# Shifting the tiles between two MLP matrices inside their buffers, and streaming half of them backward into TensorE

## The chip, the cores and the metric

The kernel runs on one core of one Trainium2 chip. The metric is the device time of one execution in microseconds; the kernel before takes 642.31 us (median of 3 runs, 641.87 to 642.67). TensorE (PE) multiplies, VectorE (DVE) and ScalarE (ACT) do elementwise work, GpSimd (POOL) helps, SyncE (SP) issues the DMAs. SBUF is the on-chip memory that all engines read, PSUM the one that TensorE writes.

## The reference, cut to what matters

Three stages run one after the other on a batch of 2 with 448 positions and 768 channels: capped softmax attention (12 heads of 64), then a Fourier mixing with a residual, a layer norm and an MLP, then a gated MLP over positions. The change lies in the MLP of the second stage alone:

```
X = np.fft.fft(np.fft.fft(x, axis=1), axis=2)
u = x + np.real(X)
un = (u - mean(u)) / sqrt(var(u) + 1e-6)
ch = np.maximum(un @ w_ch1, 0.0) @ w_ch2      # 768 -> 3072 -> 768
x = u + ch
```

## The kernel before

All activations are kept transposed: channels on the 128 partitions, the 448 positions of one batch as columns. A channel vector of 768 is six such tiles. Products are made to float32 accuracy out of a pair of tiles in the type fp32r, a high part and a low part: `product` (L134) issues three matmuls for each chunk of the contraction, high by high, high by low and low by high. In each of them the weights are the stationary operand (128 by 128) and the activations the moving one, which is streamed column by column: 448 columns. Every matmul has its own weight load (LDWEIGHTS).

The MLP has 3072 hidden channels, 24 chunks of 128. They are done in six groups `g` of four chunks (`GF = 4`). For one group, `hidden(b, g, ...)` (L719) makes the four hidden chunks of batch `b`: 18 matmuls each into PSUM (`h<-un,w` in the trace). From PSUM, ACT writes the high part with the ReLU (L727), and DVE the low part (L728), into a tile `h` of 2 by 512 columns of which the first 448 are used. Then `mixed(b, g, ...)` (L731) multiplies: for each of the six output chunks `c`, 12 matmuls with `h` as the moving operand and a block of the second matrix as weights (`c<-h,w`), into one PSUM tile of 512 columns, and DVE adds the 448 used columns to the residual (L736). `b` is 0 or 1, so a group has 144 matmuls `h<-un,w` and 144 matmuls `c<-h,w`. `hidden` and `mixed` serve the groups 1 to 5. Group 0 goes through `hidden_parts` and `mixed_parts` (L741 to L778), which are written out by hand between the Fourier stage and the layer norm of batch 1, and which have their own tiles `h`.

The order in each group is: `hidden` of batch 0, `hidden` of batch 1, `mixed` of batch 0, `mixed` of batch 1 (L1131 to L1162). Outside the written-out parts a scheduler places the instructions. The tiles `h` have four buffers for each batch, that is one group's worth. Weights come by DMA as raw 64-bit words (L670) and are converted on ACT and DVE (L685 to L693) and split into high and low parts (L131, L132) while TensorE works on the group before.

Other streams that the prediction reads: the f32 (not fp32r) products of attention, `o<-e,v` (L556) and `den<-e,ones` (L567); the f32 products of the Fourier stage, `st<-t,fold` (L221), whose moving operand is a table of three rows of 194 columns, so that its streams begin at columns 0, 194 and 388; the gate's `v<-wv,x` with 256 moving columns (L140); DVE's reversed copy `back<-pq` (L232), which reads 768 columns with step -1; and the four additions of the Fourier stage (L249 to L252), of which L250 and L252 walk through `xT` with step -1 and begin at column 1 of the PSUM tile, while L249 and L251 go forward.

Of the kernel before, what the change touches and what calls it, by code (L numbers as in the profile page):

```python
# [13 lines left out]
F32R = mybir.dt.float32r  # L14
# [7 lines left out]
P = 128  # L22
B, H, S, D = 2, 12, 448, 64
# [7 lines left out]
GF = NF // NG  # L31
# [25 lines left out]
W_BUFS = {"wa": 4, "wb": 4, "wc": 2}  # L57


FILL = {"const": 160, "wb": 96, "normed0": 224, "hidden0": 96, "wc": 96}  # L60
EDGE, GATE_ROW, TABLE_ROW = 160, 192, 3776

# [23 lines left out]
def f32(ap):  # L86
    return ap.bitcast(F32)
# [3 lines left out]
def attention_mixers_kernel(ctx, tc, bounded, q, k, v, cap, w_ch1, w_ch2, w_in, g_ln, w_sg, b_sg, w_out,  # L91
# [10 lines left out]
    def fill(pool, name):  # L102
        t = pool.tile([P, FILL[name] // 4], F32, tag="fill", bufs=1, name=f"fill_{name}")
        nc.gpsimd.memset(t[:, 0:1], 0.0)
# [4 lines left out]
    def big_ps(name):  # L109
        pool, n = banks[-1]  # L110
        return pool.tile([P, 2, 512], F32, tag="big", bufs=n, name=name)
# [3 lines left out]
    def one_ps(name):  # L115
        if not ring:
            return banks[-1][0].tile([P, 512], F32, tag="one", bufs=4, name=name)
        ring.append(ring.pop(0))
        pool, tag, n = ring[-1]
        return pool.tile([P, 512], F32, tag=tag, bufs=n, name=name)  # L120
# [8 lines left out]
    def split(hi, lo, src, lo_engine=None, hi_copy=None):  # L129

        (hi_copy or act.copy)(hi, src)  # L131
        (lo_engine or vec).tensor_tensor(lo, src, f32(hi), op=ALU.subtract)  # L132

    def product(ps, lhs, rhs, n, start=True, stop=True):  # L134

        last = 3 * n - 1
        m = 0
        for i in range(n):
            for a, b in ((0, 0), (0, 1), (1, 0)):
                pe.matmul(ps, lhs(i, a), rhs(i, b), start=start and m == 0, stop=stop and m == last)  # L140
                m += 1
# [572 lines left out]
    def rows(src, f0, name, tag="wb", **how):  # L714

        return weight(f"{name}{f0}", row_block(src, f0), 1, C, tag, **how)


    def hidden(b, g, un, w1, hs, chunks=range(GF)):  # L719
        for f0 in chunks[::2]:  # L720
            ps = big_ps(f"h{b}_{g}_{f0}")
            for i in range(2):
                product(ps[:, i, :S], lambda n, a: w1[f0 + i][:, a, n, :], lambda n, a: un[b][:, a, n, :], NP)
                yield
            for i in range(2):
                h = hpool[b].tile([P, 2, 512], F32R, tag="h", bufs=4, name=f"h{b}_{g}_{f0 + i}")[:, :, :S]
                act.activation(h[:, 0], ps[:, i, :S], AF.Relu)  # L727
                vec.scalar_tensor_tensor(h[:, 1], ps[:, i, :S], 0.0, f32(h[:, 0]), op0=ALU.max, op1=ALU.subtract)  # L728
                hs.append(h)

    def mixed(b, g, hs, w2, x2):  # L731
        u = xT[b]
        for c in range(NP):
            ps = one_ps(f"c{b}_{g}_{c}")
            product(ps[:, :S], lambda n, a: w2[n][:, a, c * P:(c + 1) * P], lambda n, a: hs[n][:, a, :], GF)
            vec.tensor_tensor(u[:, c, :], u[:, c, :], ps[:, :S], op=ALU.add)  # L736
            if x2 is not None:
                split(x2[:, 0, c, :], x2[:, 1, c, :], u[:, c, :])
            yield

    def hidden_parts(b, g, un, w1, hs):  # L741

        ps = {}

        def prod(f, rows=range(NP), idles=0):

            if f not in ps:
                t = big_ps(f"h{b}_{g}_{f}")
                stream(t[:, 0], idles)
                for i in range(2):  # L750
                    ps[f + i] = t[:, i, :S]
            for n in rows:
                product(ps[f], lambda _, a: w1[f][:, a, n, :], lambda _, a: un[b][:, a, n, :], 1,
                        start=n == 0, stop=n == NP - 1)

        def relu(f):
            h = hpool[b].tile([P, 2, 512], F32R, tag="h", bufs=4, name=f"h{b}_{g}_{f}")[:, :, :S]
            act.activation(h[:, 0], ps[f], AF.Relu)
            vec.scalar_tensor_tensor(h[:, 1], ps[f], 0.0, f32(h[:, 0]), op0=ALU.max, op1=ALU.subtract)
            hs.append(h)  # L760

        return SimpleNamespace(prod=prod, relu=relu)
# [103 lines left out]
    def opened(*names):  # L866
        pools = [ctx.enter_context(tc.tile_pool(name=name, bufs=1)) for name in names]
        for pool, name in zip(pools, names):
            if name in FILL:
                fill(pool, name)  # L870
# [15 lines left out]
    with ExitStack() as fctx:  # L886
# [8 lines left out]
        with ExitStack() as actx:  # L895
# [6 lines left out]
            w1, w2, w1_next = [], [], []  # L902
            side = iter(())
            if bounded:
                f, n0 = fourier(0, fp, t2sb, POOL_FOLDS[0]), layer_norm(0, fp)
# [83 lines left out]
        hpool = [None, None]  # L989
# [13 lines left out]
        if bounded:  # L1003
            normed[0] = opened("normed0")
            with tc.manual_schedule():
# [5 lines left out]
                hs = []  # L1011
# [69 lines left out]
                h = hidden_parts(1, 0, un, w1, hs1)  # L1081
# [19 lines left out]
        else:  # L1101
# [3 lines left out]
            def main_steps():  # L1105
                hs = []
                yield from hidden(0, 0, un, w1, hs)
                yield from mixed(0, 0, hs, w2, None)
                yield from hidden(0, 1, un, w1_next, hs_next[0], range(2))
# [11 lines left out]
    if not bounded:  # L1121
        hpool[1] = ctx.enter_context(tc.tile_pool(name="hidden1", bufs=1, side="right"))
        run(hidden(1, 0, un, w1, hs1))
    if not bounded:
        run(mixed(1, 0, hs1, w2, None))
# [5 lines left out]
    for g in range(1, NG):  # L1131
        if g == 1:
# [3 lines left out]
            hs = hs_next  # L1136
# [3 lines left out]
        else:  # L1140
            w1 = [columns(w_ch1, g * GF + f, "w1_") for f in range(GF)]
            hs = [[], []]
            for b in range(B):
                run(hidden(b, g, un, w1, hs[b]))
        if g == 3:
            for c in range(NT):
                sg_raw = sp_pool.tile([P, S], F32, tag="sgraw", bufs=1, name=f"sg_raw{c}")[:CP]
                sp.dma_start(sg_raw, w_sg[c * CP:(c + 1) * CP, :])
                ps = one_ps(f"sgT{c}")
# [8 lines left out]
        w2 = [rows(w_ch2, g * GF + f, "w2_") for f in range(GF)]  # L1158
        for b in range(B):
            if g == NG - 1:  # L1160
                x2[b] = normed[b].tile([P, 2, NP, S], F32R, tag="normed", name=f"x2_{b}")
            run(mixed(b, g, hs[b], w2, x2[b]))  # L1162
# [54 lines left out]
```

## Time and profile before

| | |
|---|---|
| median of 3 runs (lowest, highest) | 642.31 us (641.87, 642.67) |
| span of the profiled execution, first to last instruction | 641.1 us |
| PE busy | 621.4 us, 97% |
| weight loads (PEld) busy | 536.5 us, 84% |
| DVE busy | 502.7 us, 78% |
| ACT busy | 273.5 us, 43% |
| POOL busy | 82.9 us, 13% |
| `h<-un,w`, 864 matmuls | 175.3 us of PE |
| `c<-h,w`, 864 matmuls | 175.4 us of PE |

The profiled execution is known by its span alone; the three timed runs are others. Their median lies 1.2 us over the span, which is taken for what lies around the first and the last instruction. Weight loads overlap matmuls, so PE and PEld don't add up. The trace gives a matmul's start as measured, and its end as modelled: a duration of 363 ns is longer than the distance to the next start. The rate of a stream is therefore read from the chain of waits, where a stretch of so many matmuls in a row has one length.

### The profile page before, as it was taken

Reading aid. Unit: us, or ns where it says so; the run is one execution under the profiler, and the core shown is the slowest. Engines: PE = TensorE matmul, PEld = TensorE weight load, DVE = VectorE, ACT = ScalarE, POOL = GpSimd, SP = SyncE. Lnnn points to the kernel's source line nnn. Section 1 sums busy time; section 2 is a strip of 40 time slices with the busy share of each in tenths; the row PEclk is TensorE's granted clock in tenths of the full one; section 3 lists DMA queues with packets and bytes.
Section 4 is the critical chain, followed back from the end, with each engine's and each line's share of the span. In section 5 each row is a group of like instructions: output and inputs, shape, how many; then the busy total and the mean of one; then the engine's idle time right before and its main releaser. Section 6 shows DMA issues by size and latency. Waiting matters only on the chain.

```text
span 641.1 us, 8759 instructions
## 1 busy us (share of the span) xinstructions
PE 621.4 (97%) x3414; PEld 536.5 (84%) x3414; DVE 502.7 (78%) x733; ACT 273.5 (43%) x374; POOL 82.9 (13%) x82
## 2 busy tenths in 40 slices
PE   7899999999999999999999999999999999999995
PEld 5444576559988999999999989999999999999995
DVE  1899999989985789998957882698589789997451
ACT  3998875671312244333403530352245244533121
POOL 1555564353000000000000000000000000101000
PEclk9999999999999999999999999999999999999998
DMA  6754820400401144544522360145054214000123
GB/s 164 185 135 102 244 61 15 139 0 2 147 2 28 50 147 154 174 157 138 167 99 70 128 204 32 48 151 173 23 153 143 99 50 149 1 1 1 44 58 78
DMA packets 69618, 62.74 MB, mean 98 GB/s; under 512 B 35840, under 2 KB 63296, under 8 KB 69568
## 3 DMA queue, kind: packets, MB, share of 16 engines
q1 hardware_dynamic: 68640, 61.86, 31.9%
q8 instruction: 29, 0.48, 0.3%
q10 hardware_dynamic: 928, 0.23, 0.2%
q14 instruction: 21, 0.17, 0.1%
HBM read 59.32 MB, written 2.75 MB: 97 GB/s over the span
## 4 chain that ended last, share of the span: by engine, by line
PE 83%; DVE 10%; DMA 2%; ACT 2%; issue 1%; POOLq 0%; POOL 0%; DVEq 0%; ACTq 0%; SPq 0%
PE c L140 26%; PE h L140 24%; PE v L140 5%; PE out L140 5%; PE u L140 4%; PE s L532 4%; PE o L556 4%; PE sg L140 3%; DVE r L576 2%; PE st L242 1%; DMA sg_raw<-in_moe_w_sg 1%; PE st L221 1%; PE tr L501 1%; ACT e L537 1%; PE idle L152 1%
## 5 line engine op out<-in xcount | busy, mean ns | idle before, releaser
L140 PE MATMUL h<-un,w 128*128 128x448 f32 x864 | 175.3, 363 | 0.5 <-DVE un L325 0.5
L140 PE MATMUL c<-h,w 128*128 128x448 f32 x864 | 175.4, 363 | 0.0
L140 PEld LDWEIGHTS h<-un,w 128*128 128x128 f32 x864 | 161.7, 188 | 12.4 <-DVE un L325 0.8
L140 PEld LDWEIGHTS c<-h,w 128*128 128x128 f32 x864 | 161.9, 188 | 11.1 <-issue 0.4
L736 DVE TENSOR_TENSOR xT<-xT,c 128x448 f32<-128x448 f32 x60 | 36.9, 617 | 37.2 <-PE c L140 37.2
L820 POOL TENSOR_TENSOR bag<-bag,neg_half 112x1 f32<-112x1 f32 x8 | 6.0, 745 | 396.5 <-DVE bag L819 396.5
L537 ACT ACTIVATE e<-s,tanh_scale 128x896 f32<-128x896 f32 (+1 forms) x48 | 41.1, 921 | 19.6 <-PE s L532 19.2
L556 PE MATMUL o<-e,v 128*64 128x448 f32 x192 | 41.1, 551 | 0.0
L541 ACT ACTIVATE e<-e,cap_pos 128x1792 f32<-128x1792 f32 (+1 forms) x24 | 37.7, 1620 | 0.0
L140 PE MATMUL v<-wv,x 128*112 128x256 f32 x288 | 34.2, 280 | 0.0
L140 PEld LDWEIGHTS v<-wv,x 128*112 128x112 f32 x288 | 34.1, 175 | 0.1
L727 ACT ACTIVATE h<-h 128x448 fp32r<-128x448 f32 x40 | 21.7, 542 | 28.7 <-DVE h L728 19.8
L532 PE MATMUL s<-qT,kT 64*128 64x448 f32 x216 | 27.5, 383 | 6.3 <-DVE qT L510 5.2
L576 DVE RECIPROCAL r<-den 128x448 f32<-128x448 f32 x11 | 32.4, 2948 | 0.8 <-PE den L569 0.7
L532 PEld LDWEIGHTS s<-qT,kT 64*128 64x128 f32 x216 | 19.3, 185 | 16.1 <-DVE qT L510 6.9
L140 PE MATMUL out<-gated,wo 128*128 128x448 f32 x144 | 30.8, 367 | 0.0
L140 PE MATMUL u<-x,wu 128*128 128x448 f32 x144 | 29.1, 362 | 0.0
L548 POOL TENSOR_TENSOR t<-t,e 128x896 f32<-128x896 f32 x12 | 28.6, 2381 | 0.8
L140 PEld LDWEIGHTS u<-x,wu 128*128 128x128 f32 x144 | 27.0, 188 | 1.8
L545 POOL TENSOR_TENSOR t<-e 128x896 f32<-128x896 f32 x12 | 27.8, 2320 | 2.7 <-POOL mix L521 1.7
L140 PEld LDWEIGHTS out<-gated,wo 128*128 128x128 f32 x144 | 26.4, 188 | 1.8 <-ACT res L861 0.2
L556 PEld LDWEIGHTS o<-e,v 128*64 128x64 f32 x192 | 11.8, 136 | 17.6 <-issue 15.2
(380 smaller groups left out, 900.7 us busy)
## 6 DMA issues: line engine op xcount, KB each, us to landing
k<-in_k SPq DMA_DIRECT2D x24, 112.0 KB, 2.8
out<-res SPq DMA_DIRECT2D x12, 224.0 KB, 2.5
q<-in_q SPq DMA_DIRECT2D x22, 112.0 KB, 2.8
t<-dft_channels SPq DMA_DIRECT2D x8, 291.0 KB, 5.1
v<-in_v SPq DMA_DIRECT2D x24, 96.0 KB, 2.3
w_0raw<-in_moe_w_ch SPq DMA_DIRECT2D x2, 768.0 KB, 5.0
w_1raw<-in_moe_w_ch SPq DMA_DIRECT2D x2, 768.0 KB, 6.0
w_2raw<-in_moe_w_ch SPq DMA_DIRECT2D x2, 768.0 KB, 4.7
```

The source lines that it names most:

```text
L140: pe.matmul(ps, lhs(i, a), rhs(i, b), start=start and m == 0, stop=stop and m == last)
L152: pe.matmul(ps[:, 0:2 * P], idle[:, 0:P], idle, start=True, stop=True)
L221: pe.matmul(ps[:HS, m * 256:m * 256 + NE], fold[:, i, m * HS:(m + 1) * HS], tab[:, i, :], start=i == 0, stop=i == 2)
L532: pe.matmul(ps[:, i, :S], t[lo:hi, x, at:at + P], qT[lo:hi, y, :], start=m == 0, stop=m == 2)
L537: act.activation(es[n][:, 2 * step:2 * step + nr], sums.pop((n, step))[:, :nr, :S], AF.Tanh, scale=tanh_scale)
L541: act.activation(part, part, AF.Exp, scale=cap_pos)
L545: pool.tensor_tensor(t, es[n][:, 0:2], es[n][:, 2:4], op=ALU.add)
L548: pool.tensor_tensor(ts[n], ts[n], es[n][:, 4:6], op=ALU.add)
L556: pe.matmul(os[n][halfs[j], :S], vts[n % 3][:, j, i], es[n][:, 2 * i + j if i < 3 else 6], start=i == 0, stop=i == 3)
L576: vec.reciprocal(r, den[:, :S])
L727: act.activation(h[:, 0], ps[:, i, :S], AF.Relu)
L736: vec.tensor_tensor(u[:, c, :], u[:, c, :], ps[:, :S], op=ALU.add)
```

## The change

Two edits, in `hidden` and in `mixed`, thus in the groups 1 to 5.

First, a tile `h` of group 1 or later no longer starts at column 0 of its 512. A table of twenty numbers gives the starting column by group and chunk: 0, 4, 8 and so on to 60 in steps of four for the first sixteen, then 2, 6, 1 and 18 for the four chunks of group 5. Both batches use the same numbers. ACT and DVE write the tile there and TensorE reads it there. A column has 4 bytes.

Second, for batch 1 of the groups 1 to 5 both the moving operand and the PSUM output of the matmuls `c<-h,w` are addressed from the last column to the first, with step -1. Each result lands where it did before.

```
+H_AT = (0, 4, 8, 12, 16, 20, 24, 28, 32, 36, 40, 44, 48, 52, 56, 60, 2, 6, 1, 18)
...
             for i in range(2):
-                h = hpool[b].tile([P, 2, 512], F32R, tag="h", bufs=4, name=f"h{b}_{g}_{f0 + i}")[:, :, :S]
+                at = H_AT[GF * (g - 1) + f0 + i] if g else 0
+                h = hpool[b].tile([P, 2, 512], F32R, tag="h", bufs=4, name=f"h{b}_{g}_{f0 + i}")[:, :, at:at + S]
                 act.activation(h[:, 0], ps[:, i, :S], AF.Relu)
                 vec.scalar_tensor_tensor(h[:, 1], ps[:, i, :S], 0.0, f32(h[:, 0]), op0=ALU.max, op1=ALU.subtract)
...
             ps = one_ps(f"c{b}_{g}_{c}")
-            product(ps[:, :S], lambda n, a: w2[n][:, a, c * P:(c + 1) * P], lambda n, a: hs[n][:, a, :], GF)
+            back = -1 if b and g else 1
+            product(ps[:, :S][:, ::back], lambda n, a: w2[n][:, a, c * P:(c + 1) * P],
+                    lambda n, a: hs[n][:, a, ::back], GF)
             vec.tensor_tensor(u[:, c, :], u[:, c, :], ps[:, :S], op=ALU.add)
```

No instruction moves on any engine: DVE, ACT, POOL and SP have the same instructions in the same order with the same waits. On TensorE the matmuls stand in the same order too, and 11 places get a wait on TensorE's own semaphore (`PE_49`). Nine are the first matmuls of output chunks 1, 2 and 3 of batch 0 in the groups 2, 4 and 5; two are transposes of the gate's matrix in group 3. Here is TensorE in the program before, where `mixed` of batch 0 in group 2 begins its second output chunk (`c0_2_1` is batch 0, group 2, chunk 1; the names end in a running number):

```order
L140 MATMUL c0_2_0_2690<-h0_2_3_2557,w2_11_2682 128x448 x2
L140 MATMUL c0_2_1_2704<-h0_2_0_2511,w2_8_2649 128x448 x3
L140 MATMUL c0_2_1_2704<-h0_2_1_2514,w2_9_2660 128x448 x3
L140 MATMUL c0_2_1_2704<-h0_2_2_2554,w2_10_2671 128x448 x3
L140 MATMUL c0_2_1_2704<-h0_2_3_2557,w2_11_2682 128x448 x3
L140 MATMUL c0_2_2_2718<-h0_2_0_2511,w2_8_2649 128x448 x3
```

The same place now (the line is L141, since the table added one):

```order
L141 MATMUL c0_2_0_2690<-h0_2_3_2557,w2_11_2682 128x448 x2
L141 MATMUL c0_2_1_2704<-h0_2_0_2511,w2_8_2649 128x448 [waits PE_49]
L141 MATMUL c0_2_1_2704<-h0_2_0_2511,w2_8_2649 128x448 x2
L141 MATMUL c0_2_1_2704<-h0_2_1_2514,w2_9_2660 128x448 x3
L141 MATMUL c0_2_1_2704<-h0_2_2_2554,w2_10_2671 128x448 x3
L141 MATMUL c0_2_1_2704<-h0_2_3_2557,w2_11_2682 128x448 x3
L141 MATMUL c0_2_2_2718<-h0_2_0_2511,w2_8_2649 128x448 [waits PE_49]
```

Nothing moved; the first matmul of a chunk has a wait. It waits for the last user of the same PSUM tile on TensorE, a chunk of `mixed` of batch 1 in the group before, which stands more than 140 matmuls earlier.

## Rows read from the trace of the kernel before

**Rows 1.** Head of the page: busy time of each engine, TensorE's slices and clock

```profile
PE 621.4 (97%) x3414; PEld 536.5 (84%) x3414; DVE 502.7 (78%) x733; ACT 273.5 (43%) x374; POOL 82.9 (13%) x82
...
PE   7899999999999999999999999999999999999995
...
PEclk9999999999999999999999999999999999999998
```

**Rows 2.** Chain of waits in order of time: start, length (us), what, how many

```profile
255.37 28.80 PE c L140 x144
284.17 28.91 PE h L140 x144
313.08 28.80 PE c L140 x144
341.88 28.81 PE h L140 x144
371.11 2.89 DMA sg_raw<-in_moe_w_sg
...
431.53 28.80 PE c L140 x144
460.33 28.81 PE h L140 x144
489.14 28.80 PE c L140 x144
...
532.36 16.92 PE v L140 x144
```

**Rows 3.** Stretches of the groups 2 to 5: length, busy (count) by engine, clock, DMA

```profile
284.00:342.00 58.00, 58.00 (x291) 54.20 (x290) 44.46 (x65) 18.08 (x26) 0.00 (x0) 1.00 0.38 125
460.00:518.00 58.00, 58.00 (x292) 54.38 (x291) 47.33 (x72) 23.68 (x36) 0.00 (x0) 1.00 0.35 109
```

**Rows 4.** Costliest groups on TensorE: count, busy us, mean ns, idle before

```profile
L140 PE MATMUL c<-h,w 128*128 128x448 f32 x864 | 175.4, 363 | 0.0
L140 PE MATMUL h<-un,w 128*128 128x448 f32 x864 | 175.3, 363 | 0.5 <-DVE un L325 0.5
```

**Rows 5.** TensorE's Fourier products, three starting columns: ns min/median/max, first and last start

```profile
L221 PE MATMUL st<-t,fold x96: 325/327/420, 81.8 to 165.6; 128*113 128x194 f32 x96
```

**Rows 6.** The slower streams of 448 columns on TensorE, columns as in rows 4

```profile
L567 PE MATMUL den<-e,ones 128*64 128x448 f32 x48 | 11.2, 544 | 0.4 <-DVE r L576 0.4
```

**Rows 7.** DVE forward and with step -1, columns as in rows 5

```profile
L131 DVE CAST w<-w_1cvt x1: 552/552/552, 42.4 to 42.4; 128x768 fp32r<-128x768 f32 x1
...
L232 DVE COPY back<-pq x4: 550/553/2440, 99.8 to 168.1; 113x768 f32<-113x768 f32 x4
...
L249 DVE TENSOR_TENSOR xT<-xT,st x12: 376/380/393, 102.2 to 177.2; 128x225 f32<-128x225 f32 x12
...
L250 DVE TENSOR_TENSOR xT<-xT,st x12: 373/378/381, 102.5 to 177.5; 128x223 f32<-128x223 f32 x12
```

**Rows 8.** What ACT and DVE do to the tiles `h`, columns as in rows 5

```profile
L727 ACT ACTIVATE h<-h x40: 517/545/557, 235.6 to 490.7; 128x448 fp32r<-128x448 f32 x40
L728 DVE SCALAR_TENSOR_TENSOR h<-h,h x40: 615/617/625, 237.0 to 491.7; 128x448 fp32r<-128x448 f32 x40
```

**Rows 9.** A semaphore instruction of TensorE's queue, columns as in rows 5

```profile
L221 PEldq EVENT_SEMAPHORE  x8: 51/51/2537, 80.9 to 161.5; - x8
```

## Prediction

> **What bounds the kernel now.** Read the head of the page first: TensorE is busy for 621.4 of 641.1 us, its slices are full from the second on, and the granted clock is full in all of them but the last [rows 1]. Then read the chain of waits in order of time. In the MLP it holds nothing but TensorE: 144 matmuls of `h<-un,w`, 144 of `c<-h,w`, and so on, 28.8 us each, broken only by three short waits for a DMA in group 3 [rows 2]. [...] So in groups 1 to 5 the time is the number of matmuls by the distance from one start to the next, and anything that ACT or DVE do has spare time. The distance is 28.80 us / 144 = 200.0 ns for `c<-h,w` and 28.81 / 144 = 200.1 ns for `h<-un,w` [rows 2]. Over the whole kernel the two kinds are alike too: 175.4 and 175.3 us for 864 each [rows 4].
>
> **The change part by part.** It removes and moves nothing. What it alters is how an operand is addressed. I take five parts.
>
> *Streams that start elsewhere.* In five groups there are 5 x 144 = 720 matmuls `c<-h,w`. One start of twenty is still column 0, so 684 read from a shifted column, with the same 448 columns and the same weights. No row has an fp32r stream with such a start. The nearest is `st<-t,fold`: a table of three rows of 194 columns, so a third of its 96 streams each starts at column 0, 194 and 388; 194 is even but no multiple of four. Their durations are 325 at the least, 327 in the median [rows 5], and a stalled start would show here, because the 420 does. Half of all lie within 2 ns of the least although two thirds start off column 0. I take 0. For the bounds I use two fp32r rows: 256 columns take 16.92 us / 144 = 117.5 ns, 448 take 200.0 [rows 2], so a column costs 82.5 / 192 = 0.430 ns, and 117.5 - 256 x 0.430 = 7.4 ns are left per matmul beside the columns. At best a better start takes all of that away: 684 x 7.4 ns = -5.1 us. At worst it is paid a second time: +5.1 us.
>
> *The one tile at column 1.* Of the starts 2, 6, 1 and 18 only the 1 is odd: 3 matmuls by 6 chunks by 2 batches = 36. If columns went to TensorE in aligned pairs, these would fall apart. The slowest 448-column stream in the trace has a mean of 544 ns against 363 [rows 4, 6], so +181 ns; at worst 36 x 181 ns = +6.5 us, at best 0 (already in the -5.1). I take 0: DVE's additions that begin at column 1 of PSUM take 378 ns for 223 columns, those from column 0 take 380 for 225 [rows 7]. It is another engine, so the upper end stays in mind.
>
> *Streams that run backward.* Batch 1 has 5 x 72 = 360 of them, 360 x 200.0 ns = 72.0 us of the chain. Moving operand and output both have step -1. No row shows TensorE with a negative step, so this is the unknown that matters. Below: 0, since the columns are the same number and the stretch is already 448 columns at 0.430 ns plus 7.4. Above: the slow stream's +181 ns on each, 360 x 181 ns = +65.2 us. The nearest rows with a negative step are DVE's. Its reversed copy of 768 columns takes 553 ns in the median and 550 at the least, the forward one of as many 552 [rows 7]. 552 / 768 = 0.72 ns per column, well under the 617 / 448 = 1.38 of a DVE pass that reads PSUM [rows 8], so this is a fast path, and step -1 doesn't lose it. The additions with step -1 through `xT` tie with the forward ones as well [rows 7]. I take 0.
>
> [...]
>
> *Writes of the tiles.* 40 times ACT writes a shifted tile and 40 times DVE does, 545 and 617 ns [rows 8]. An odd start may cost something there. What covers it: the last tile of batch 0 is written while batch 1's 72 matmuls `h<-un,w` run, that of batch 1 while batch 0's 72 `c<-h,w` run, 72 x 0.2 = 14.4 us each, and a PSUM tile of two chunks is wanted back only after the other one's 36 matmuls, 7.2 us. Doubled to 1.1 and 1.2 us they would still be hidden. Cost 0; without the cover, 40 x 0.55 us would show at most for each doubling, 22 us on ACT.
>
> *Waits on TensorE's own semaphore.* 11 waits, each for a matmul more than 140 places back, thus 140 x 0.2 = 28 us old. Behind a waiting matmul all of TensorE stands, and behind it DVE's addition; but the value is long there. An instruction of TensorE's queue for a wait takes 51 ns when it need not wait [rows 9]. Two of the places, the transposes, wait for a DMA anyway [rows 2]. At most 11 x 51 ns = 0.6 us, at least 0; since the queue runs ahead of the matmuls, I take 0.1.
>
> **Sum.** 0 + 0 + 0 + 0 + 0.1 us on the profiled span: 641.1 + 0.1 = 641.2. The median of the runs shown is 642.31, 1.2 us over that span, so 642.4.
>
> **Rivals.**
>
> *Rival 1, slower by much: backward streams run at half rate.* Place: the 72.0 us of batch 1's `c<-h,w`. Mechanism: TensorE takes or writes two neighbouring columns at once and does so only upward, so that each column becomes an access of its own. Price up to 360 x 181 ns = 65.2 us: 642.3 + 65.2 = 707.5. It decides from 1.28 us / 360 = 3.6 ns per backward matmul. [...] Against it: DVE's fast copy, which keeps its rate backward [rows 7].
>
> *Rival 2, slower by a little: a start or a turn has a fixed price.* Every shifted stream pays up to another 7.4 ns: 642.4 + 5.1 = 647.5, with the middle at 645. A backward stream that only begins late belongs here too: 15 ns on 360 are 5.4 us, the same size. It decides from 1.28 / 684 = 1.9 ns per shifted matmul. For it: no fp32r row has a start like these, and the odd one may cost 6.5 us alone. Against it: the even 325 to 327 ns of `st<-t,fold` [rows 5].
>
> *Rival 3, faster: the present starts are the bad ones.* Tiles and weights at like places could get in each other's way, and twenty different starts would break that up. All of the 7.4 ns gone on 684 matmuls is 5.1 us: 642.3 - 5.1 = 637.2. For it: 7.4 ns that no column explains. Against it: `un` and `h` are different tiles in different pools with the same 200.0 and 200.1 ns [rows 2], so where a tile lies has not mattered so far.
>
> **How the numbers follow.** No change 0.63, rival 1 0.12, rival 2 0.15, rival 3 0.10. A difference under 0.2% (1.28 us) can't be told from none here. So faster 0.10, same 0.63, slower 0.12 + 0.15 = 0.27. The likeliest case's own range is 641.0 to 643.6. The range given is 639.5 to 647.7: it holds no change, rival 2 to its end and half of rival 3, together about 0.83, and leaves out rival 1, whose price lies far off.
>
> **What would show it.** Right: in the chain of waits the stretches of 144 `c<-h,w` in groups 1 to 5 stay at 28.8 us, TensorE stays at 58.00 of 58.00 with clock 1.00, and no new wait of TensorE for itself is listed. Rival 1: such a stretch grows to some 40 us, and its second half, batch 1, has starts near 380 ns apart while the first half keeps 200. Rival 2: both halves grow by a few ns each, or only the 36 matmuls of the odd tile in group 5 do. Rival 3: both halves fall towards 193 ns. The writes at L727 and L728 should keep 545 and 617 ns. I am wrong if TensorE's distances in batch 1's half differ from 200 ns by 4 or more, or if TensorE waits where it did not.

## The result, and the profile after

The changed kernel takes 645.73 us (median of 3 runs, 645.70 to 646.15) against 642.31 us before: 1.0057 of the time, 95% interval 1.0037 to 1.0076, thus 3.4 us slower. The profiled execution has a span of 643.5 us.

The costliest groups on TensorE, columns as in rows 4:

```profile
L141 PE MATMUL c<-h,w 128*128 128x448 f32 x864 | 178.8, 367 | 0.0
L141 PE MATMUL h<-un,w 128*128 128x448 f32 x864 | 175.2, 362 | 1.5 <-DVE d L322 1.0
```

They answer to [rows 4]: `h<-un,w` keeps its 175 us, `c<-h,w` has 3.4 us more, with no idle time before it. The chain of waits shows where; start, length in us, what, how many:

```profile
227.43 28.81 PE h L141 x144
256.24 29.35 PE c L141 x144
285.59 28.81 PE h L141 x144
314.40 29.55 PE c L141 x144
343.94 28.81 PE h L141 x144
...
383.18 26.00 PE c L141 x127
...
433.60 29.45 PE c L141 x144
463.05 28.80 PE h L141 x144
491.85 29.69 PE c L141 x144
521.54 14.40 PE u L141 x72
```

Three more lines of the chain before, for comparison here and below (batch 1 of group 0, the 127 of group 3, the first `u`):

```profile
212.15 14.40 PE c L140 x72
...
381.69 25.43 PE c L140 x127
...
517.95 14.41 PE u L140 x72
```

Beside [rows 2], every stretch of 144 `c<-h,w` has grown: by 0.55, 0.75, 0.65 and 0.89 us in groups 1, 2, 4 and 5; the 127 of group 3 took 25.43 us before, +0.57. That makes 3.41 us, as much as the medians differ (3.42). The two profiled spans differ by 2.4 us only: the changed one reaches group 1's `c<-h,w` 0.9 us later, spends 0.6 us less on the waits between the two stretches of group 3, and ends 1.2 us sooner after its last ACT instruction. These three lie outside the stretches of `c<-h,w`, and no run ties them to the change. `h<-un,w` stays at 28.8. In a stretch the first 72 matmuls are batch 0 (forward), the last 72 batch 1 (backward). Worked out from the start of each matmul (in group 3 without the places where a wait cuts in), the mean distances are 201.7, 204.8, 203.3, 203.8 and 205.1 ns in batch 0 of groups 1 to 5, and 206.0, 205.6, 205.5, 205.3 and 207.2 ns in batch 1, against 200.0 in all ten before. Summed over 72 matmuls each: 1.3 us from batch 0, 2.1 us from batch 1. Both parts of the change cost, and both by a few ns per matmul.

Two stretches that answer to [rows 3], groups 2 and 5, then the writes of the tiles [rows 8]:

```profile
285.60:343.60 58.00, 58.00 (x288) 53.74 (x288) 42.37 (x62) 17.92 (x25) 0.00 (x0) 1.00 0.36 123
463.50:521.50 58.00, 58.00 (x287) 53.79 (x286) 46.58 (x71) 23.18 (x35) 0.00 (x0) 1.00 0.32 109
```

```profile
L729 ACT ACTIVATE h<-h x40: 521/546/556, 236.2 to 493.4; 128x448 fp32r<-128x448 f32 x40
```

```profile
L730 DVE SCALAR_TENSOR_TENSOR h<-h,h x40: 615/618/625, 237.6 to 494.4; 128x448 fp32r<-128x448 f32 x40
```

TensorE waits for nobody and its clock is full, but in 58 us it starts 3 and 5 matmuls fewer than before. ACT and DVE write the shifted tiles as fast as ever.

### The profile page after: what moved, and what is told of

The parts are those of the page before. It is cut to its first block, busy times and chain, and to the rows that moved or that the text cites. A ratio compares the mean times of both kernels' runs of the same rounds, so it can differ in the third digit from the quotient of the medians.

```text
span 643.5 us, 8761 instructions
## 1 busy us (share of the span) xinstructions
PE 624.5 (97%) x3414; PEld 536.4 (83%) x3414; DVE 504.0 (78%) x733; ACT 274.1 (43%) x374; POOL 82.5 (13%) x82
## 4 chain that ended last, share of the span: by engine, by line
PE 84%; DVE 10%; ACT 2%; DMA 1%; issue 1%; POOLq 0%; POOL 0%; DVEq 0%; ACTq 0%; SPq 0%
PE c L141 26%; PE h L141 24%; PE v L141 5%; PE out L141 5%; PE u L141 4%; PE s L533 4%; PE o L557 4%; PE sg L141 3%; DVE r L577 2%; PE st L243 1%; PE st L222 1%; PE tr L502 1%; DVE xT L578 1%; ACT e L538 1%; PE xt L863 1%
## 5 line engine op out<-in xcount | busy, mean ns | idle before, releaser
L141 PE MATMUL c<-h,w 128*128 128x448 f32 x864 | 178.8, 367 | 0.0
L141 PE MATMUL h<-un,w 128*128 128x448 f32 x864 | 175.2, 362 | 1.5 <-DVE d L322 1.0
L141 PEld LDWEIGHTS c<-h,w 128*128 128x128 f32 x864 | 162.3, 188 | 14.1 <-issue 0.4
L141 PEld LDWEIGHTS h<-un,w 128*128 128x128 f32 x864 | 161.7, 187 | 13.4 <-DVE d L322 1.8
L729 ACT ACTIVATE h<-h 128x448 fp32r<-128x448 f32 x40 | 21.7, 544 | 30.2 <-DVE h L730 18.7
L141 PE MATMUL v<-wv,x 128*112 128x256 f32 x288 | 34.2, 280 | 0.0
L141 PEld LDWEIGHTS v<-wv,x 128*112 128x112 f32 x288 | 34.1, 175 | 0.1
L141 PE MATMUL out<-gated,wo 128*128 128x448 f32 x144 | 30.8, 366 | 0.0
L141 PE MATMUL u<-x,wu 128*128 128x448 f32 x144 | 29.1, 362 | 0.0
L141 PEld LDWEIGHTS u<-x,wu 128*128 128x128 f32 x144 | 26.9, 187 | 1.8
L141 PEld LDWEIGHTS out<-gated,wo 128*128 128x128 f32 x144 | 26.4, 188 | 1.8 <-ACT res L865 0.2
```

## The experiments

The first four take the change apart. `shift_only` keeps the starts and turns nothing; `back_only` keeps the turning and starts all tiles at column 0:

```
 shift_only:   back = 1
 back_only:    H_AT = (0,) * 20
```

> The twenty starts stay, nothing runs backward. If the shifted starts have a price of their own (theory A), both batches show what batch 0 shows in the changed kernel: stretches of 144 matmuls c<-h,w of 29.1 to 29.6 us in place of 28.8, and about +2.7 us over the kernel before (720 matmuls, 3.8 ns each on average). If shift and step -1 only hurt together (theory B), the stretches keep 28.8 us and the time is that of before.

> All tiles begin at column 0, batch 1 of groups 1 to 5 runs backward. If step -1 has a price of its own (theory A), batch 1's half of each stretch is at 205 to 206 ns per matmul and batch 0's at 200.0: stretches of 29.2 us, +2.1 us in all (360 by 5.9 ns). If step -1 costs only what a shifted start costs (theory B), it is 200.0 ns in both halves and the time of before.

`shift_only` ran in 1.0034 of the time of the kernel before (1.0021 to 1.0046, 2.2 us), `back_only` in 1.0040 (1.0026 to 1.0053, 2.6 us). The chains, shifts alone first, then turning alone:

```profile
254.75 29.04 PE c L141 x144
312.59 29.51 PE c L141 x144
...
431.79 29.35 PE c L141 x144
489.95 29.53 PE c L141 x144
```

```profile
254.50 29.27 PE c L141 x144
312.59 29.29 PE c L141 x144
...
431.48 29.28 PE c L141 x144
489.57 29.29 PE c L141 x144
```

Each has a price of its own (theory A). With shifts alone, both batches run at nearly the distances that batch 0 shows in the changed kernel. With turning alone, batch 0 is at 200.0 to 200.2 ns and batch 1 at 206.5 to 206.6, the same in every group and a little over the 205 to 206 expected: 72 x 6.55 ns = 0.47 us, the 29.27 of a stretch. The two don't add up in batch 1: in the chains it is 3.41 us together, not 2.5 + 2.4, since a shifted stream that also runs backward is at 205 to 207 ns as well.

`same_starts` gives the four tiles of a group one start, forward; `one_side` turns only one of the two operands:

```
 same_starts:  H_AT = (16,) * 4 + (8,) * 4 + (4,) * 4 + (2,) * 4 + (1,) * 4;  back = 1
 one_side:     H_AT = (0,) * 20
               into  = -1 if b and g in (3, 4, 5) else 1     # PSUM output
               along = -1 if b and g in (1, 2, 3) else 1     # tile h
```

> All forward; within a group the four tiles share one start: 16, 8, 4, 2 and 1 columns in groups 1 to 5. If the price is that of where a stream starts (theory C), each group shows its own: a start 64 bytes on (16) at 200.0 ns, the finer ones at 203 to 206. If the price is that of neighbouring streams with different starts (theory D), all five groups keep 200.0 ns, but for the first matmul of each chunk.

> No shifts. In batch 1, groups 1 and 2 read the tile backward and write PSUM forward, group 3 does both backward, groups 4 and 5 read forward and write PSUM backward; where only one side is turned, DVE reads PSUM from the last column. If the price lies in reading SBUF (theory E), batch 1 is at 205 to 206 ns in groups 1 to 3 and 200.0 in 4 and 5. If it lies in writing PSUM (theory F), it is 200.0 in groups 1 and 2 and 205 to 206 in 3 to 5.

`same_starts` took 645.41 us in a single run. Its chain, groups 1, 2, 4 and 5:

```profile
255.42 29.37 PE c L141 x144
313.60 29.58 PE c L141 x144
...
433.00 29.76 PE c L141 x144
491.58 29.77 PE c L141 x144
```

That is 204.0, 205.4, 206.7 and 206.7 ns for starts of 16, 8, 2 and 1 columns; column 4 in group 3 is at 203.3. So theory D falls: neighbours with the same start pay too. But theory C does not come out as worded either: a start 64 bytes on was to be free and costs 4.0 ns, while the odd column costs no more than column 2. `one_side` took 643.45 us in a single run:

```profile
254.98 29.27 PE c L141 x144
313.06 29.29 PE c L141 x144
...
432.00 28.80 PE c L141 x144
489.62 28.80 PE c L141 x144
```

Groups 1 and 2 read backward and pay as in `back_only` (batch 1 at 206.5 to 206.6 ns), groups 4 and 5 write PSUM backward and pay nothing. The price lies in reading SBUF (theory E): with the PSUM output alone at step -1 the stretches keep 28.80 us.

If it is not a matter of neighbouring streams, it may be one of what else TensorE reads at that time: the weights of the next matmul. In the trace of before such a load takes 188 ns in the mean for `c<-h,w`, and it runs beside the matmuls: in the 58.00 us of group 2 in the changed kernel, loads are busy for 53.74 us and matmuls for all of it. In the built program before, each tile `h` lies 64 bytes past a multiple of 256 bytes and each block of the second matrix on a multiple of 256, and the same distance of 64 (modulo 256) stands between `un` and the first matrix, and between the streams and the weights of `u`, of `out` and of `sg`. The next four runs tell place from distance:

```
 weights_moved: H_AT = (0,) * 20;  back = 1
                FILL = {... "wb": 160, "normed0": 160 ...}    # was 96 and 224
 both_moved:    H_AT = (16,) * 20;  back = 1;  the same FILL
 ten_starts:    H_AT = ((12, 20), (24, 28), (32, 36), (40, 48), (56, 64));  back = 1
                at = H_AT[g - 1][b] if g else 0
 ten_back:      H_AT = ((4, 8), (12, 16), (24, 32), (40, 48), (56, 63));  back = -1 if g else 1
                at = H_AT[g - 1][b] if g else 0
```

> No shifted start and nothing backward; the second matrix's tiles lie 64 bytes further in SBUF (two fillers of unused bytes, one longer by 64, the next shorter by 64), the tiles h where they were. If a stream's price goes by where it begins relative to the weights that are loaded beside it (theory G), c<-h,w loses 200.0 ns and comes to about the 203.8 of the stream shifted by 64 bytes, some +2.7 to +5 us in all. If it goes by where the stream begins in SBUF (theory H), c<-h,w keeps 200.0 ns and the time is that of before.

> The second matrix's tiles lie 64 bytes further and the tiles h of groups 1 to 5 begin at column 16, which is 64 bytes too, so the distance between the two is that of before. Theory G (relative to the weights): 200.0 ns in groups 1 to 5. Theory H (where the stream begins): 203.8 to 204.1 ns, as with column 16 alone.

> All forward; each batch of each group has one start for its four tiles: 12 and 20, 24 and 28, 32 and 36, 40 and 48, 56 and 64 columns in batches 0 and 1 of groups 1 to 5. If the price comes from two readers that meet in SBUF (theory G), it repeats with the distance: one or more of the ten are back at 200 ns, 64 columns (256 bytes) most likely, and the others lie between 200 and 207. If leaving column 0 has a price as such (theory I), all ten are at 203 to 207.

> Both batches of groups 1 to 5 run backward, each with one start for its tiles: 4 and 8, 12 and 16, 24 and 32, 40 and 48, 56 and 63 columns. If a stream that runs backward is only another way of meeting the weight loads (theory G), some of the ten starts come down to 200 to 204 ns. If step -1 has a fixed price (theory J), all ten are at 206.5 ns.

One run of each gave 645.05, 641.45, 645.11 and 645.85 us, beside 641.34 for one of the kernel before. The first two were then run several times each:

> The second matrix's tiles 64 bytes further, the tiles h where they were, timed. Theory G: 202.7 to 206.6 ns for 864 matmuls c<-h,w, +2 to +5.7 us; if the level that a distance settles at is fixed by the program, the stretches are 29.18 us again, and if it varies from run to run (theory K), some stretch has another length than in the look before. Theory H: the time of before.

> The second matrix's tiles 64 bytes further, the tiles h of groups 1 to 5 at column 16, timed. Theory G (distance between stream and weights): 200.0 ns again in groups 1 to 5, and the time of before within 0.1% (group 0, whose tiles stay at column 0, may pay some 0.2 to 0.5 us). Theory H (place of the stream alone): +2.7 us or more.

`weights_moved_timed`: 1.0045 of the time before (1.0029 to 1.0060). `both_moved_timed`: 1.0011 (1.0001 to 1.0020). The chain with the weights alone moved, from group 0 on:

```profile
212.86 14.87 PE c L141 x72
...
256.54 29.18 PE c L141 x144
...
314.52 29.18 PE c L141 x144
...
433.70 29.18 PE c L141 x144
...
491.69 29.18 PE c L141 x144
```

and with stream and weights moved by the same 64 bytes:

```profile
212.34 14.59 PE c L141 x72
...
255.74 28.80 PE c L141 x144
...
313.37 28.81 PE c L141 x144
...
431.82 28.80 PE c L141 x144
...
489.44 28.81 PE c L141 x144
...
573.59 17.01 PE v L141 x144
```

Streams that nobody touched lose 2.6 ns per matmul when only their weights move (29.18 / 144 = 202.6), and a start at column 16, which cost 4.0 ns alone, is free when the weights have moved along. That is theory G, and theory H (place alone) falls. What `both_moved_timed` still loses, 0.7 us by the ratio (0.1 to 1.3), has rows for 0.4: group 0, whose tiles stay at column 0 while the weights move, takes 14.59 us for the 72 of batch 1 where it took 14.40, 48 of batch 0 pay 0.1 us, and the gate's `v<-wv,x`, whose moving tiles share the second matrix's buffers, takes 17.01 us for 144 the second time where it took 16.92.

`ten_starts`, the mean distance of each start, forward: 12: 206.6, 20: 206.4, 24: 206.6, 28: 204.2, 32: 202.2, 36: 204.0, 40: 204.4, 48: 206.6, 56: 206.5, 64: 200.1 ns. Column 64, 256 bytes on, is the one that is free, as theory G had it; theory I falls. `ten_back`, backward: 204.4 for 4, 24, 32, 40 and 56, and 206.5 to 206.7 for 8, 12, 16, 48 and 63. So backward has no fixed price (theory J falls), but none of eleven backward starts reached 200, and the 204.4 is a little over the 204 up to which theory G let some of them come down. In all, no start tried is faster than 200.0. Two stretches of each show it, `ten_starts` with columns 40 and 48, then 56 and 64, and `ten_back` with columns 12 and 16, then 40 and 48:

```profile
433.12 29.60 PE c L141 x144
...
491.52 29.28 PE c L141 x144
```

```profile
313.92 29.75 PE c L141 x144
...
433.51 29.59 PE c L141 x144
```

In the 29.28 the 72 matmuls of column 56 take 72 x 206.5 ns = 14.87 us, which leaves 14.41 for column 64.

Last, the theory carried to streams that the change left alone. The kernel before, with a filler of 64 bytes in front of the first matrix's tiles and the next filler shorter by as much:

```
 first_moved:  FILL = {... "wa": 64, "wb": 32 ...}   # was none and 96
```

> The kernel before with the tiles of the first matrix, the gate's u weights and the output weights 64 bytes further (the second matrix and all streams stay). Theory G, carried to streams that the change did not touch: h<-un,w goes from 200.1 to between 202.6 and 206.7 ns for 792 of 864 matmuls, and so do u and out, 1080 matmuls in all, +2.8 to +7.1 us; the first two chunks of group 1, whose weights lie in another pool and are not moved, keep 200 ns, and c<-h,w keeps 28.8 us per 144. If only the tiles h matter (theory L), nothing changes.

It ran in 1.0074 of the time of before (1.0058 to 1.0090, 4.8 us):

```profile
227.99 28.99 PE h L140 x144
256.98 28.81 PE c L140 x144
285.79 29.18 PE h L140 x144
314.98 28.81 PE c L140 x144
...
409.54 25.20 PE h L140 x122
434.74 28.81 PE c L140 x144
463.55 29.19 PE h L140 x144
...
521.53 14.59 PE u L140 x72
```

Now `h<-un,w` pays, `u` pays (14.59 for 14.40), `out` pays (9.91 us for 48 where it took 9.61), and `c<-h,w` keeps its 28.8. Group 1's stretch is shorter than the others since its first two chunks, whose weights lie in another pool, stay at 200.0 ns and the rest is at 202.7. Theory L falls.

Left open: how large the price is at a given distance. In `weights_moved_timed` groups 1 to 5 are at 202.6 ns and batch 1 of group 0 at 14.87 / 72 = 206.5, with the same distance; in `both_moved_timed` that batch has the same tiles and weights at the same addresses, and is at 14.59 / 72 = 202.6. In `first_moved` group 4 is at 25.20 / 122 = 206.6 and its neighbours at 202.7. Nor is a mix the mean of its parts: starts of 0, 4, 8 and 12 columns in turn, as in group 1 of the changed kernel, run at 201.7 ns, while alone they run at 200.0, 203.3, 205.4 and 206.6. The levels came again in a second run of the same program (29.18 and 14.87 in `weights_moved` too), so they look like a property of the program, but what chooses between them was not found. Nor is it shown whether, or how, the two reads meet inside the memory; shown is that the distance between stream and weights decides whether a forward stream pays (28.80 us for 144 with both moved by 64 bytes, 29.18 with the weights alone). That a backward stream pays for the same reason is not shown: its price changes with its start, but no start freed it, and no run read a weight block the other way round.

## Why the prediction was right or wrong

The range held the time (645.73 in 639.5 to 647.7), but the forecast, no change at 642.4, did not come true, and the prediction's own sign of being wrong appeared: batch 1's distances differ from 200 ns by 5.3 to 7.2, where 4 was to be enough. What came is rival 2 in sign and size, a little slower, at two thirds of the 5.1 us that it was priced at. Its mechanism, a fixed price of a start or a turn, did not come: column 64 is free (200.1 ns), and the backward streams of `ten_back` have two levels (204.4 and 206.5 to 206.7 ns). Tiles and weights that get in each other's way were rival 3's mechanism, there with the opposite sign. So the range held by the width of its bounds, which is luck as far as the cause goes.

*What bounds the kernel:* right. The loss is the number of matmuls by the growth of their distance, 3.41 us in the chain, and TensorE waits for nothing new in those stretches.

*Streams that start elsewhere, taken at 0:* wrong, within its bounds (-5.1 to +5.1 us). Measured: 1.3 us in batch 0, 2.5 us if both batches run forward. The step failed on its stand-in. `st<-t,fold` is an f32 stream of 194 columns, and its even 325 to 327 ns [rows 5] said that starts off column 0 don't matter to it; for the fp32r streams they do (202.2 to 206.7 ns alone, but for column 64). The 7.4 ns of the bounds are no clean remainder either, since the row of 256 columns has weights of 112 columns and not 128:

```profile
L140 PE MATMUL v<-wv,x 128*112 128x256 f32 x288 | 34.2, 280 | 0.0
```

*The one tile at column 1, taken at 0:* right that an odd start is nothing special, wrong that it is free. Alone, columns 1 and 2 both run at 206.7 ns.

*Streams that run backward, taken at 0:* wrong. 6.55 ns on each, 2.4 us alone and 2.1 us in the changed kernel; the upper bound of 65.2 us was far off, and rival 1 with it: no batch that ran backward had a mean over 207.2 ns. DVE's copies [rows 7] showed that step -1 kept the rate there (553 and 552 ns), and nothing of the distance between two reads. Of the two operands turned, only the tile in SBUF costs (29.27 and 29.29 us for 144 against 28.80).

*Writes and waits, taken at 0 and 0.1 us:* right. L729 and L730 keep their times (546 and 618 ns), and TensorE lists no new wait on itself: in group 2's batch 0 the three output chunks that begin with a new wait and the two behind them all run at 205.0 ns.

*Rival 3's counter-argument:* this is where the trace was misread. "`un` and `h` are different tiles in different pools with the same 200.0 and 200.1 ns [rows 2], so where a tile lies has not mattered so far" took two equal rates for proof that place is free. Both streams stand 64 bytes (modulo 256) from their own weights. The rates were equal because the distance was, and it is the best of all distances tried; so the present starts were not the bad ones but the good ones, and every move but the one by 256 bytes cost.

## What to carry to other kernels

Two streams with one rate don't show that a property is without effect unless they differ in it: look up what they share, addresses included. In this kernel, where TensorE runs back to back and each matmul loads its own weights, the place of the moving tile against the stationary one in SBUF is worth up to 3% of a matmul (206.7 against 200.0 ns); so shift both by the same amount (64 bytes on both kept 28.80 us for 144) or neither, and look at a stretch of a hundred matmuls in the chain of waits, where 3 ns on each are plain. Other types and sizes of matmul were not tried. The PSUM output ran backward for nothing (28.80 us for 144 in `one_side`).

## What the runs showed that was not expected

A matmul with 448 fp32r columns, streamed forward, took 200.0 ns from start to start where the tile lay 64 or 320 bytes (modulo 512) past its weights, and 202.2 to 206.7 ns at every other distance that was tried by itself. With the streams untouched, moving the weights by 64 bytes cost 2.6 ns on each matmul (29.18 us for 144 in place of 28.80), and moving the streams along gave it back (28.80). No start made a stream faster than 200.0 ns.
